# A one-token attention and FFN kernel: query weights at the front in long rows, another order for the K and V loads, and most of the output projection ahead of the last V blocks

## The chip, the cores and the metric

The kernel runs on one core of a Trainium2 chip. The metric is the device time of one execution in microseconds (us). Executions of a kernel agree here within some tenths of a per cent, so times are medians of several runs. A profile is one execution, and its span is some 2 us shorter than the time that is measured around it.

A 128 x 128 block product on PE (TensorE) is a pair of instructions: a weight load (PEld in the profile) and a matmul. DVE is VectorE, ACT is ScalarE, POOL is GpSimd, and SP is the sequencer that issues the loads.

## The reference

One token goes through grouped-query attention over a cache of 32768 positions and through a gated FFN, and a gate mixes the two.

```python
# x: 1 x 512; K and V caches: 8 groups x 32768 positions x 128 (64 MB each in bf16)
g = sigmoid((x * gate_w).sum(-1))
q = (x @ wq).reshape(32, 128)                 # 32 heads, 4 for each of 8 K/V groups
p = softmax(q @ k.T * 128 ** -0.5)            # for each head, k of its group
a = (p @ v).reshape(4096) @ wo                # wo: 4096 x 512
b = (silu(x @ w_gate) * (x @ w_up)) @ w_down  # 512 -> 1792 -> 512
out = g * a + (1 - g) * b
```

There is little arithmetic for each byte: 148 MB are read once, 134 MB of them K and V.

## The kernel before

K and V come in 128 blocks of 1 MB (4096 positions; each partition gets 32 positions, one row of 8 KB). PE transposes each K block, DVE and ACT copy the transposes to SBUF, and PE multiplies them with the four queries of the group. When a group's scores are complete, the maximum is taken (DVE, then an all-partition reduction on POOL), ACT exponentiates, and V blocks of that group are multiplied while the next group's K runs.

One list of jobs gives both the order of the loads and the order of the work on PE. In a group, four K blocks (six in the last) come before V starts:

```python
NKB = 5        # K buffers
NVB = 6        # V buffers
def vlag(g):
    return 6 if g == G - 1 else 4
# ... jobs: K(g,0..VL-1), then V(g-1,b) and K(g,b) in turn, then what is left of V(g-1)
jobs += [("V", G - 1, b) for b in range(NB)]
# on SP, for each job in turn:
if kind == "K":
    if b == 0:
        issue_wq(g)                            # 0.5 MB: this group's 512 columns, rows of 1 KB
    if ki >= NKB:
        sp.wait_ge(sem_fill, FPB * (ki - NKB + 1))
    sp.dma_start(kbuf[:, slot, :, :], ...)     # 1 MB
    if g == 0 and b == 3:
        issue_wf()                             # w_gate, w_up, w_down
else:
    if not wo_issued and g == G - 1:
        sp.wait_ge(sem_pe_b, 1)                # w_o overwrites the FFN weights
        sp.dma_start(wo_v, A_wo.rearrange("(h p) n -> p h n", p=128))
    ...
```

At the end, everything after the last V block is serial:

```python
pe.matmul(ps_e[:, 0:H], ones_f, esum2)         # sums of the exponentials over the partitions
# DVE: rS = 1 / ps_e;  oTs = ps_o * rS
for oc in range(OC):                           # 4 x 32 matmuls with w_o
    for h in range(H):
        pe.matmul(ps_m[:, M_A0 + oc : ...], wo_v[:, h, oc * 128 : (oc + 1) * 128], oTs[:, h : h + 1])
# DVE: diff = a - b; res = g * diff + b;  PE: 4 transposes to a row;  DVE: copy;  SP: store
```

## Time and profile before

| | before |
|---|---|
| time, median | 381.31 us |
| span of the profile | 379.5 us |
| PE busy, mean granted clock | 73%, 0.752 |
| read from HBM | 148.11 MB, 390 GB/s over the span |
| packets under 2 KB | 12230 of 29696 |
| last V block landed | 370.3 us |
| from there to the end | 9.1 us |

The page of the kernel before, in part: its first line, the row of PE's share, two rows of forty slices of the span (DMA busy in tenths, and GB/s), the packets, the queues, and the chain of waits that ended last.

```profile
span 379.5 us, 14143 instructions
...
PE 278.0 (73%) x6582; PEld 271.5 (72%) x6582; DVE 139.0 (37%) x233; ACT 99.9 (26%) x210; POOL 4.3 (1%) x17
...
DMA  7999999999999999999999999999999899999960
GB/s 283 401 381 417 407 420 415 419 405 417 419 420 412 414 415 421 413 408 421 415 421 406 418 419 418 414 408 420 419 416 410 359 376 421 415 366 383 420 273 4
DMA packets 29696, 149.02 MB, mean 393 GB/s; under 512 B 2243, under 2 KB 12230, under 8 KB 13254
...
q1 hardware_dynamic: 29638, 148.12, 96.3%
q8 instruction: 52, 0.85, 0.9%
...
DMA 44%; PE 40%; issue 11%; DVE 2%; SPq 1%; ACT 0%; POOL 0%; POOLq 0%
```

DMA is full from the second slice nearly to the end, so this is a kernel of loads. The tempting lines are the low slices (359 and 376 near 300 us). The windows by stage of the kernel before look at them closer; the columns are the stretch, the busy time of each engine with its instructions, the clock of PE, the DMA share of sixteen engines, and GB/s.

```profile
295.00:300.00 5.00, 1.88 (x51) 1.71 (x52) 0.00 (x0) 0.00 (x0) 0.00 (x0) 0.50 1.01 413
300.00:305.00 5.00, 5.00 (x87) 5.00 (x85) 2.47 (x5) 1.02 (x1) 0.00 (x0) 0.62 0.65 259
305.00:310.00 5.00, 4.93 (x123) 4.84 (x121) 4.96 (x10) 3.11 (x17) 0.37 (x1) 1.00 0.98 393
```

On average a third of the DMA engines stand idle from 300 to 305 us. In the last group six K loads are issued in a row into five buffers, and the sixth waits until PE has emptied the first. Whether that costs time is decided by another record of the trace: each large load's 16 landings, read here as one for each DMA engine. The table is made from those records (us from the span's start; "step" is the time since the last landing of the load before).

```
load    first   8th     13th    last    step of the last
K(0,0)    7.03    7.35    7.54    7.76
K(3,0)  125.20  128.14  128.57  130.07  3.81
K(3,1)  127.69  130.60  131.06  132.58  2.50
K(7,3)  297.67  302.42  305.85  307.19  2.55
K(7,4)  300.15  304.90  308.33  309.68  2.49
K(7,5)  308.40  308.94  310.82  312.18  2.49     <- 8.25 us after K(7,4), not 2.49
V(6,0)  310.89  311.42  314.57  314.85  2.68
w_o     345.22  345.74  348.90  349.17 11.90     4 MB
V(7,6)  362.71  363.15  366.39  367.84  2.48
V(7,7)  365.18  365.61  368.87  370.31  2.47
```

The landings of one load drift apart, from 0.7 us to 9.5 us. A load counts only when the last one is in. The last engine takes 2.49 us for each 1 MB load, with some longer steps like the 3.81, but it never stops: while the early engines stand idle for some 5.8 us (their landings of K(7,4) and K(7,5) are 8.25 us apart in place of 2.49), its step stays at 2.49 us.

The tail in the timeline of the kernel before (start, duration, engine, line, operation, tiles; in brackets the idle time before it):

```profile
370.36 1.02 PE L468 MATMUL ps_o<-ET,vbuf 128*128 128x4 bf16 x32 [1.45 <-DMA vbuf<-in_A_v_cache_dram]
...
371.24 0.61 PE L484 MATMUL pst<-esum,ones_f 128*128 128x32 f32 x2
371.89 0.36 DVE L658 RECIPROCAL rS<-pst 128x32 f32<-128x32 f32 x1 [37.88 <-PE pst L484]
372.28 0.19 DVE L661 TENSOR_TENSOR oTs<-ps_o,rS 128x32 bf16<-128x32 f32 x1
...
372.52 3.57 PE L495 MATMUL ps_m<-oTs,wfo 128*128 128x1 bf16 x128 [0.68 <-DVE oTs L661]
...
377.24 0.68 DVE L679 CAST res_row<-pst 1x512 bf16<-1x512 f32 x1 [0.68 <-PE pst L505]
377.94 0.27 SPq L323 DMA_DIRECT2D out_dram<-res_row  x1
```

PE is ready and waits 1.45 us for the last V block. Then 9.1 us of small steps follow, of which the 128 matmuls with w_o are the largest.

### The profile page before, as it was taken

To read this page: it belongs to the slowest core of one execution; us is meant where nothing else is said; L and a number is where in the kernel's file an instruction comes from. 1 tells how busy PE (TensorE), PEld (TensorE's weight loads), DVE (VectorE), ACT (ScalarE), POOL (GpSimd) and SP (SyncE) were. 2 spreads that over 40 slices of the span, in tenths; PEclk is the share of its full clock that TensorE was granted. 3 is DMA by queue.
4 is the path that set the end of the run, shared out by engine and by line. 5 is a ranking of instruction groups with operands and counts; after the bars stand their busy time and mean duration, and the time that the engine had idled before them with its cause. 6 is when DMAs were issued, how large, how long until landed. Compare 5 with 4: busy or idle time off the path is not lost.

```text
span 379.5 us, 14143 instructions
## 1 busy us (share of the span) xinstructions
PE 278.0 (73%) x6582; PEld 271.5 (72%) x6582; DVE 139.0 (37%) x233; ACT 99.9 (26%) x210; POOL 4.3 (1%) x17
## 2 busy tenths in 40 slices
PE   0469969886988698859898598958985697840345
PEld 0468969786988698859898598858985597830235
DVE  0226536330933184306722184205731194300001
ACT  1035561331533043403232143203332143410000
POOL 0000000000000000000000000000000000000000
PEclk9959967985988689966956598556987599855555
DMA  7999999999999999999999999999999899999960
GB/s 283 401 381 417 407 420 415 419 405 417 419 420 412 414 415 421 413 408 421 415 421 406 418 419 418 414 408 420 419 416 410 359 376 421 415 366 383 420 273 4
DMA packets 29696, 149.02 MB, mean 393 GB/s; under 512 B 2243, under 2 KB 12230, under 8 KB 13254
## 3 DMA queue, kind: packets, MB, share of 16 engines
q1 hardware_dynamic: 29638, 148.12, 96.3%
q8 instruction: 52, 0.85, 0.9%
q14 instruction: 6, 0.05, 0.0%
HBM read 148.11 MB, written 0.00 MB: 390 GB/s over the span
## 4 chain that ended last, share of the span: by engine, by line
DMA 44%; PE 40%; issue 11%; DVE 2%; SPq 1%; ACT 0%; POOL 0%; POOLq 0%
DMA kbuf<-in_A_k_cache_dram 35%; PE pst L449 24%; DMA vbuf<-in_A_v_cache_dram 10%; PE ps_sc L416 7%; PE ps_o L468 6%; SPq L314 1%; DVE ktT L627 1%; PE ps_m L495 1%; PE ps_m L368 1%; DVE pmaxf L609 0%; PE ps_m L381 0%; PE ps_m L354 0%; ACT ktT L552 0%; DVE res_row L679 0%; PE pst L505 0%
## 5 line engine op out<-in xcount | busy, mean ns | idle before, releaser
L449 PE MATMUL pst<-ident,kbuf 128*128 128x128 bf16 x2048 | 189.6, 247 | 24.0 <-ACT ktT L552 10.1
L627 DVE COPY ktT<-pst 128x1024 bf16<-128x1024 bf16 x188 | 125.3, 690 | 179.8 <-PE pst L449 179.6
L449 PEld LDWEIGHTS pst<-ident,kbuf 128*128 128x128 bf16 x2048 | 143.1, 111 | 27.1 <-issue 14.3
L552 ACT ACTIVATE ktT<-pst 128x1024 bf16<-128x1024 bf16 x68 | 69.6, 1024 | 190.1 <-PE pst L449 190.1
L468 PE MATMUL ps_o<-ET,vbuf 128*128 128x4 bf16 x2048 | 63.6, 168 | 49.7 <-DMA vbuf<-in_A_v_cache_dram 40.4
L416 PE MATMUL ps_sc<-qT,ktT 128*128 128x4 bf16 x2048 | 92.6, 167 | 6.2 <-issue 6.1
L468 PEld LDWEIGHTS ps_o<-ET,vbuf 128*128 128x128 bf16 x2048 | 58.9, 99 | 52.0 <-DMA vbuf<-in_A_v_cache_dram 28.3
L416 PEld LDWEIGHTS ps_sc<-qT,ktT 128*128 128x128 bf16 x2048 | 86.9, 102 | 6.2 <-issue 5.9
L536 ACT ACTIVATE ET<-ps_sc,nbias 128x128 bf16<-128x128 f32 x64 | 22.5, 377 | 0.2
L658 DVE RECIPROCAL rS<-pst 128x32 f32<-128x32 f32 x1 | 0.4, 357 | 37.9 <-PE pst L484 37.9
L536 ACT ACTIVATION_READ_ACCUMULATOR ET<-ps_sc,nbias 128x1 f32 x64 | 13.8, 216 | 0.0
L354 PE MATMUL ps_m<-xT,wqb 128*128 128x1 bf16 x128 | 4.8, 166 | 11.6 <-POOL ident L239 7.0
L354 PEld LDWEIGHTS ps_m<-xT,wqb 128*128 128x128 bf16 x128 | 4.1, 103 | 12.2 <-POOL ident L239 7.1
L609 DVE TENSOR_REDUCE pmaxf<-ps_sc 128x4 f32<-128x512 f32 x16 | 10.9, 681 | 0.4 <-PE ps_sc L416 0.4
L528 ACT ACTIVATE nbias<-gmax 128x4 f32<-128x4 f32 x8 | 1.6, 205 | 22.9 <-POOL gmax L254 22.9
L254 POOL PARTITION_ALL_REDUCE gmax<-pmax x8 | 3.0, 374 | 306.2 <-DVE pmax L613 306.2
L517 ACT ACTIVATE g_col<-gtot 128x1 f32<-128x1 f32 x1 | 0.2, 202 | 19.4 <-POOL gtot L249 19.4
L368 PE MATMUL ps_m<-xT,wfo 128*128 128x1 bf16 x112 | 3.2, 164 | 2.5 <-issue 2.5
L368 PEld LDWEIGHTS ps_m<-xT,wfo 128*128 128x128 bf16 x112 | 3.0, 99 | 2.6 <-issue 2.6
L495 PEld LDWEIGHTS ps_m<-oTs,wfo 128*128 128x128 bf16 x128 | 3.5, 104 | 0.8 <-DVE oTs L661 0.8
L495 PE MATMUL ps_m<-oTs,wfo 128*128 128x1 bf16 x128 | 3.6, 165 | 0.7 <-DVE oTs L661 0.7
L585 DVE CAST qT<-ps_m 128x4 bf16<-128x4 f32 x8 | 1.2, 153 | 7.0 <-PE ps_m L354 7.0
(36 smaller groups left out, 16.9 us busy)
## 6 DMA issues: line engine op xcount, KB each, us to landing
kbuf<-in_A_k_cache_dram SPq DMA_DIRECT2D x64, 1024.0 KB, 17.1
vbuf<-in_A_v_cache_dram SPq DMA_DIRECT2D x64, 1024.0 KB, 17.9
wqb<-in_A_wq_dram SPq DMA_DIRECT2D x8, 512.0 KB, 17.2
wfo<-in_A_wo_dram SPq DMA_DIRECT2D x1, 4096.0 KB, 23.3
wfo<-in_B_w_gate_dram SPq DMA_DIRECT2D x1, 1792.0 KB, 17.1
wfo<-in_B_w_up_dram SPq DMA_DIRECT2D x1, 1792.0 KB, 21.1
wfo<-in_B_w_down_dram SPq DMA_DIRECT2D x1, 1792.0 KB, 25.6
x_row<-in_A_x_dram SPq DMA_DIRECT2D x1, 1.0 KB
```

The costliest lines, as they stand in the source:

```text
L254: pool.partition_all_reduce(gmax[:, g, :], pmax[:, g, :], 128, ReduceOp.max).then_inc(sem_gmax, 1)
L314: sp.dma_start(vbuf[:, slot, :, :], A_v_cache[0, g, b * B : (b + 1) * B, :].rearrange("(p r) d -> p r d", r=R),).then_inc(sem_v_load[slot] ...
L354: ins = pe.matmul(ps_m[:, M_Q0 + h : M_Q0 + h + 1], wqb[:, slot, c, hl * DH : (hl + 1) * DH], xT[:, c : c + 1], start=(c == 0), stop=(c == ...
L368: ins = pe.matmul(ps_m[:, base + fc : base + fc + 1], wt[:, c, fc * 128 : (fc + 1) * 128], xT[:, c : c + 1], start=(c == 0), stop=(c == KC ...
L416: ins = pe.matmul(bank[:, col : col + HPG], ktT[:, slot, t * 128 : (t + 1) * 128], qT[:, g * HPG : (g + 1) * HPG], start=True, stop=True,)
L449: ins = pe.transpose(stb[:, t * 128 : (t + 1) * 128], kbuf[:, slot, r, :], ident[:, :],)
L468: ins = pe.matmul(ps_o[:, g * HPG : (g + 1) * HPG], vbuf[:, slot, r, :], ET[:, g, :, n], start=(n == 0), stop=(n == NT - 1),)
L495: ins = pe.matmul(ps_m[:, M_A0 + oc : M_A0 + oc + 1], wo_v[:, h, oc * 128 : (oc + 1) * 128], oTs[:, h : h + 1], start=(h == 0), stop=(h == ...
L536: act.activation(ET[:, g, h, bk * TPSB : (bk + 1) * TPSB], sc[:, h, :], ACT.Exp, bias=nbias[:, g, h : h + 1], scale=SCALE, accum_out=esum[ ...
L552: act.activation(ktT[:, j % NKT, :], pst[j % NST][:, :], ACT.Copy).then_inc(sem_cp_a, 1)
L609: dve.tensor_reduce(pmaxf[:, f, :], sc, AX.X, ALU.max).then_inc(sem_pmax, 1)
L627: dve.tensor_copy(ktT[:, j % NKT, :], pst[j % NST][:, :]).then_inc(sem_cp_d, 1)
```

## The change

Its intent: larger pieces for the weights that come in 1 KB rows, an order of loads that keeps more of them outstanding, and a shorter tail. Its core, with cuts:

```diff
-    NVB = 6
+    NVB = 8
     def vlag(g):
-        return 6 if g == G - 1 else 4
+        return 2
+    dma_jobs = []                      # an order of its own for the loads
+    for g in range(G):
+        for b in range(NB):
+            if g >= 1:
+                dma_jobs.append(("V", g - 1, b))
+            dma_jobs.append(("K", g, b))
+    dma_jobs += [("V", G - 1, b) for b in range(NB)]
 ...  # SP: all of wq at the front, rows of 8 KB; PE: q of all heads at once
+                for c in range(KC):
+                    sp.dma_start(wq_v[:, c, :], A_wq[c * 128 : (c + 1) * 128, :])
 ...  # w_down in rows of 14 KB; the FFN's columns are dealt to match
-                        wd, B_w_down.rearrange("(c p) n -> p c n", p=128)
+                        wd, B_w_down.rearrange("(p c) n -> p c n", p=128)
-                                    wt[:, c, fc * 128 : (fc + 1) * 128],
+                                    wt[:, c, :].rearrange("p (q f) -> p q f", f=FC)[:, :, fc],
 ...  # w_o right after, into the place of wq
+                    sp.wait_ge(sem_pe_q, 1)
+                    sp.dma_start(wo_v, A_wo.rearrange("(h p) n -> p h n", p=128))
 ...  # PE, ahead of the V blocks of the last group
+                        if g == G - 1 and b == 0:
+                            emit_S(0, G - 1)              # sums of groups 0 to 6
+                            emit_wo(M_A0, 0, HE)          # 28 of 32 heads: 112 matmuls
+                        if g == G - 1 and b == 5:
+                            emit_S(G - 1, G)              # sums of group 7
                         if b == 0:
+                            pe.wait_ge(sem_exp, 2 * HPG * g + HPG)   # half of the group
+                        if b * R == TPSB:
                             pe.wait_ge(sem_exp, 2 * HPG * (g + 1))
 ...  # after the last V block only the last group's 16 matmuls are left
+                emit_wo(M_A1, HE, H)
```

To make room, the exponentials of three groups are kept (they were kept for all eight), and VectorE's part of the tail is split in the same way.

More of the change, by code (lines that the diff above doesn't have):

```diff
@@ L60, in bass_gated_mix__gqa_block_cached__swiglu_ffn__decode_kernel @@
     LAG = 3
-    NWQ = 2
+    NEG = 3
     SCALE = float(DH) ** -0.5
@@ L123, in bass_gated_mix__gqa_block_cached__swiglu_ffn__decode_kernel, with _check_orders @@
     assert len(jobs) == 2 * G * NB
+    dma_jobs = []
[5 more added lines that the diff above has]
+    dma_jobs += [("V", G - 1, b) for b in range(NB)]
+    assert sorted(dma_jobs) == sorted(jobs)
+    def _check_orders():
+        issued_k = issued_v = 0
+        cons_k = cons_v = 0
+        di = 0
+        pi = 0
+        nK = sum(1 for j in dma_jobs if j[0] == "K")
+        progress = True
+        while pi < len(jobs) and progress:
+            progress = False
+            while di < len(dma_jobs):
+                kind = dma_jobs[di][0]
+                if kind == "K" and issued_k - cons_k < NKB:
+                    issued_k += 1
+                elif kind == "V" and issued_v - cons_v < NVB:
+                    issued_v += 1
+                else:
+                    break
+                di += 1
+                progress = True
+            kind = jobs[pi][0]
+            if kind == "K" and cons_k < issued_k:
+                cons_k += 1
+                pi += 1
+                progress = True
+            elif kind == "V" and cons_v < issued_v:
+                cons_v += 1
+                pi += 1
+                progress = True
+        assert pi == len(jobs), f"static schedule deadlocks at pe job {pi} / dma job {di}"
+    _check_orders()
     with ExitStack() as es:
@@ L130, in bass_gated_mix__gqa_block_cached__swiglu_ffn__decode_kernel @@
         sem_v_load = [S_(f"s_v_load{i}") for i in range(NVB)]
-        sem_wq_load = [S_(f"s_wq_load{i}") for i in range(NWQ)]
+        sem_ld_wq = S_("s_ld_wq")
         sem_fill = S_("s_fill")
@@ L190, in bass_gated_mix__gqa_block_cached__swiglu_ffn__decode_kernel @@
         WF = 2 * KC * F + FC * NOUT
-        assert H * NOUT <= WF
         wfo = T("wfo", [128, WF], BF16)
@@ L195, in bass_gated_mix__gqa_block_cached__swiglu_ffn__decode_kernel @@
         wd = wfo[:, 2 * KC * F : WF].rearrange("p (c n) -> p c n", c=FC)
-        wo_v = wfo[:, 0 : H * NOUT].rearrange("p (h n) -> p h n", h=H)
-        wqb = T("wqb", [128, NWQ, KC, HPG * DH], BF16)
+        WQO = max(KC * H * DH, H * NOUT)
+        wqo = T("wqo", [128, WQO], BF16)
+        wq_v = wqo[:, 0 : KC * H * DH].rearrange("p (c n) -> p c n", c=KC)
+        wo_v = wqo[:, 0 : H * NOUT].rearrange("p (h n) -> p h n", h=H)
         kbuf = T("kbuf", [128, NKB, R, DH], BF16)
@@ L200, in bass_gated_mix__gqa_block_cached__swiglu_ffn__decode_kernel @@
         ktT = T("ktT", [128, NKT, TPF * 128], BF16)
-        ET = T("ET", [128, G, HPG, NT], BF16)
+        ET = T("ET", [128, NEG, HPG, NT], BF16)
         pmaxf = T("pmaxf", [128, NSB, HPG], FP32)
@@ L210, in bass_gated_mix__gqa_block_cached__swiglu_ffn__decode_kernel @@
         b_col = T("b_col", [128, OC], FP32)
+        pre_col = T("pre_col", [128, OC], FP32)
         diff_col = T("diff_col", [128, OC], FP32)
@@ L227, in bass_gated_mix__gqa_block_cached__swiglu_ffn__decode_kernel @@
         M_A0 = M_B0 + OC
-        assert M_A0 + OC <= 512
+        M_A1 = M_A0 + OC
+        M_E0 = M_A1 + OC
+        assert M_E0 + H <= 512
+        HE = H - HPG
         ps_e = pst[0][:, :].bitcast(FP32)
@@ L261, in _, with issue_weights @@
                 sp.dma_start(gw_row[0:1, :], gate_w.unsqueeze(0)).then_inc(sem_ld_x, 16)
-                def issue_wq(g):
-                    slot = g % NWQ
-                    if g >= NWQ:
-                        sp.wait_ge(sem_pe_q, g - NWQ + 1)
+                for c in range(KC):
                     sp.dma_start(
-                        wqb[:, slot, :, :],
-                        A_wq[:, g * HPG * DH : (g + 1) * HPG * DH].rearrange(
-                            "(c p) n -> p c n", p=128
-                        ),
-                    ).then_inc(sem_wq_load[slot], 16)
-                def issue_wf():
+                        wq_v[:, c, :], A_wq[c * 128 : (c + 1) * 128, :]
+                    ).then_inc(sem_ld_wq, 16)
+                def issue_weights():
                     sp.dma_start(
@@ L281, in issue_wf @@
                     sp.dma_start(
-                        wd, B_w_down.rearrange("(c p) n -> p c n", p=128)
+                        wd, B_w_down.rearrange("(p c) n -> p c n", p=128)
                     ).then_inc(sem_ld_wf, 16)
+                    sp.wait_ge(sem_pe_q, 1)
+                    sp.dma_start(
+                        wo_v, A_wo.rearrange("(h p) n -> p h n", p=128)
+                    ).then_inc(sem_ld_wo, 16)
                 ki = 0
                 vi = 0
-                wo_issued = False
-                for kind, g, b in jobs:
+                for kind, g, b in dma_jobs:
                     if kind == "K":
-                        if b == 0:
-                            issue_wq(g)
                         slot = ki % NKB
@@ L301, in _ @@
                         ki += 1
-                        if g == 0 and b == min(3, NB - 1):
-                            issue_wf()
-                    else:
-                        if not wo_issued and g == G - 1:
-                            sp.wait_ge(sem_pe_b, 1)
-                            sp.dma_start(
-                                wo_v, A_wo.rearrange("(h p) n -> p h n", p=128)
-                            ).then_inc(sem_ld_wo, 16)
-                            wo_issued = True
+                        if g == 0 and b == 3:
+                            issue_weights()
+                    else:
                         slot = vi % NVB
@@ L320, in _ @@
                         vi += 1
-                assert wo_issued and ki == G * NB and vi == G * NB
+                assert ki == G * NB and vi == G * NB
                 sp.wait_ge(sem_dve_row, 1)
@@ L340, in _ @@
                 pe.wait_ge(sem_ident, 1)
-                def emit_q(g):
-                    slot = g % NWQ
-                    pe.wait_ge(sem_wq_load[slot], 16 * (g // NWQ + 1))
-                    if g == 0:
-                        pe.wait_ge(sem_dve_x, 2)
-                    else:
-                        pe.wait_ge(sem_dve_qT, g)
-                    if g == 2:
-                        pe.wait_ge(sem_dve_bcol, 1)
-                    for hl in range(HPG):
-                        h = g * HPG + hl
-                        for c in range(KC):
-                            ins = pe.matmul(
-                                ps_m[:, M_Q0 + h : M_Q0 + h + 1],
-                                wqb[:, slot, c, hl * DH : (hl + 1) * DH],
-                                xT[:, c : c + 1],
-                                start=(c == 0),
-                                stop=(c == KC - 1),
-                            )
-                    ins.then_inc(sem_pe_q, 1)
+                pe.wait_ge(sem_dve_x, 2)
+                pe.wait_ge(sem_ld_wq, 16 * KC)
+                for h in range(H):
+                    for c in range(KC):
+                        ins = pe.matmul(
+                            ps_m[:, M_Q0 + h : M_Q0 + h + 1],
+                            wq_v[:, c, h * DH : (h + 1) * DH],
+                            xT[:, c : c + 1],
+                            start=(c == 0),
+                            stop=(c == KC - 1),
+                        )
+                ins.then_inc(sem_pe_q, 1)
                 def emit_ffn():
@@ L403, in emit_scores @@
                         sc_group_started.add(g)
-                        pe.wait_ge(sem_dve_qT, g + 1)
+                        if g == 0:
+                            pe.wait_ge(sem_dve_qT, 1)
                     wait_copy(j)
@@ L427, in emit_scores, with emit_S, emit_wo @@
                         emit_outb()
+                def emit_S(g0, g1):
+                    pe.wait_ge(sem_dve_esum2, 1 if g0 == 0 else 2)
+                    pe.matmul(
+                        ps_m[:, M_E0 + g0 * HPG : M_E0 + g1 * HPG],
+                        ones_f[:, :],
+                        esum2[:, g0:g1, :].rearrange("p g h -> p (g h)"),
+                        start=True,
+                        stop=True,
+                    ).then_inc(sem_pe_S, 1)
+                def emit_wo(base, h0, h1):
+                    pe.wait_ge(sem_dve_oTs, 1 if h0 == 0 else 2)
+                    pe.wait_ge(sem_ld_wo, 16)
+                    for oc in range(OC):
+                        for h in range(h0, h1):
+                            ins = pe.matmul(
+                                ps_m[:, base + oc : base + oc + 1],
+                                wo_v[:, h, oc * 128 : (oc + 1) * 128],
+                                oTs[:, h : h + 1],
+                                start=(h == h0),
+                                stop=(h == h1 - 1),
+                            )
+                    ins.then_inc(sem_pe_a, 1)
                 kuse = [0] * NKB
@@ L436, in _ @@
                     if kind == "K":
-                        if b == 0:
-                            emit_q(g)
                         slot = ki % NKB
@@ L470, in _ @@
                                 vbuf[:, slot, r, :],
-                                ET[:, g, :, n],
+                                ET[:, g % NEG, :, n],
                                 start=(n == 0),
@@ L481, in _ @@
                 assert next_scores == NF and vi == G * NB
-                pe.wait_ge(sem_dve_esum2, 1)
-                pe.matmul(
-                    ps_e[:, 0:H],
-                    ones_f[:, :],
-                    esum2[:, :, :].rearrange("p g h -> p (g h)"),
-                    start=True,
-                    stop=True,
-                ).then_inc(sem_pe_S, 1)
-                pe.wait_ge(sem_dve_oTs, 1)
-                pe.wait_ge(sem_ld_wo, 16)
-                for oc in range(OC):
-                    for h in range(H):
-                        ins = pe.matmul(
-                            ps_m[:, M_A0 + oc : M_A0 + oc + 1],
-                            wo_v[:, h, oc * 128 : (oc + 1) * 128],
-                            oTs[:, h : h + 1],
-                            start=(h == 0),
-                            stop=(h == H - 1),
-                        )
-                ins.then_inc(sem_pe_a, 1)
+                emit_wo(M_A1, HE, H)
                 pe.wait_ge(sem_dve_res, 1)
@@ L520, in emit_sg @@
                     act.wait_ge(sem_pe_h, 1)
-                    act.wait_ge(sem_dve_qT, 2)
+                    act.wait_ge(sem_dve_qT, 1)
                     act.activation(
@@ L531, in emit_exps @@
                     act.wait_ge(sem_nbias, g + 1)
+                    if g >= NEG:
+                        act.wait_ge(sem_v_free, NB * (g - NEG + 1))
                     for bk in range(2):
@@ L536, in emit_exps @@
                             act.activation(
-                                ET[:, g, h, bk * TPSB : (bk + 1) * TPSB],
+                                ET[:, g % NEG, h, bk * TPSB : (bk + 1) * TPSB],
                                 sc[:, h, :],
@@ L581, in _ @@
                 )
-                def emit_qcopy(g):
-                    dve.wait_ge(sem_pe_q, g + 1)
-                    dve.tensor_copy(
-                        qT[:, g * HPG : (g + 1) * HPG],
-                        ps_m[:, M_Q0 + g * HPG : M_Q0 + (g + 1) * HPG],
-                    ).then_inc(sem_dve_qT, 1)
+                dve.wait_ge(sem_pe_q, 1)
+                dve.tensor_copy(qT[:, :], ps_m[:, M_Q0 : M_Q0 + H]).then_inc(sem_dve_qT, 1)
                 def emit_t():
@@ L615, in emit_pmax @@
                         ).then_inc(sem_pmax, 1)
-                emit_qcopy(0)
                 next_f = 0
-                next_qg = 1
                 t_done = False
@@ L629, in _ @@
                         )
-                    if next_qg < G and j >= next_qg * FPG:
-                        emit_qcopy(next_qg)
-                        next_qg += 1
                     if not t_done and j >= J_DVE_T:
@@ L641, in _ @@
                         next_f += 1
-                while next_qg < G:
-                    emit_qcopy(next_qg)
-                    next_qg += 1
                 if not t_done:
@@ L651, in _, with emit_rS @@
                     next_f += 1
-                dve.wait_ge(sem_exp, 2 * HPG * G)
-                dve.tensor_tensor(
-                    esum2[:, :, :], esum[:, :, 0, :], esum[:, :, 1, :], ALU.add
-                ).then_inc(sem_dve_esum2, 1)
-                dve.wait_ge(sem_pe_S, 1)
-                dve.reciprocal(rS[:, :], ps_e[:, 0:H]).then_inc(sem_dve_rS, 1)
-                dve.wait_ge(sem_dve_rS, 1)
-                dve.wait_ge(sem_v_free, G * NB)
-                dve.tensor_tensor(oTs[:, :], ps_o[:, 0:H], rS[:, :], ALU.mult).then_inc(
+                def emit_rS(g0, g1):
+                    k = 1 if g0 == 0 else 2
+                    dve.wait_ge(sem_exp, 2 * HPG * g1)
+                    dve.tensor_tensor(
+                        esum2[:, g0:g1, :], esum[:, g0:g1, 0, :], esum[:, g0:g1, 1, :], ALU.add
+                    ).then_inc(sem_dve_esum2, 1)
+                    dve.wait_ge(sem_pe_S, k)
+                    dve.reciprocal(
+                        rS[:, g0 * HPG : g1 * HPG],
+                        ps_m[:, M_E0 + g0 * HPG : M_E0 + g1 * HPG],
+                    ).then_inc(sem_dve_rS, 1)
+                    dve.wait_ge(sem_dve_rS, k)
+                emit_rS(0, G - 1)
+                dve.wait_ge(sem_v_free, (G - 1) * NB)
+                dve.tensor_tensor(oTs[:, 0:HE], ps_o[:, 0:HE], rS[:, 0:HE], ALU.mult).then_inc(
                     sem_dve_oTs, 1
@@ L665, in _ @@
                 dve.tensor_tensor(
-                    diff_col[:, :], ps_m[:, M_A0 : M_A0 + OC], b_col[:, :], ALU.subtract
+                    pre_col[:, :], ps_m[:, M_A0 : M_A0 + OC], b_col[:, :], ALU.subtract
                 ).then_inc(sem_dve_diff, 1)
+                emit_rS(G - 1, G)
+                dve.wait_ge(sem_v_free, G * NB)
+                dve.tensor_tensor(oTs[:, HE:H], ps_o[:, HE:H], rS[:, HE:H], ALU.mult).then_inc(
+                    sem_dve_oTs, 1
+                )
+                dve.wait_ge(sem_pe_a, 2)
                 dve.wait_ge(sem_dve_diff, 1)
+                dve.tensor_tensor(
+                    diff_col[:, :], ps_m[:, M_A1 : M_A1 + OC], pre_col[:, :], ALU.add
+                ).then_inc(sem_dve_diff, 1)
+                dve.wait_ge(sem_dve_diff, 2)
                 dve.wait_ge(sem_act_g, 1)
```

## The prediction

> **What bounds the kernel now.** The DMA stream: on the page its row stands at 9 from the second slice to the 37th, queue 1 uses 96.3% of sixteen engines' span, and the chain of waits is mostly K and V loads (35% and 10%). PE is 73% busy at a mean clock of 0.752: slack. The trace's landing records say more. A load is done only when its 16 landings are in (the Trainium skill, "DMA: Bandwidth & Descriptors", section on why a DMA increments its semaphore by 16; every load here shows 16). First and last landing are 0.7 us apart at the start and drift to 9.5 us at 300 us; I put that to the 52 instruction fetches of 16 KB (1.07 us each) falling on some engines only. So the last engine sets the time. Its landings step by 2.49 us per 1 MB, without a hole, from 5 to 370.3 us. The dip in the windows by stage (300 to 305 us: 259 GB/s, DMA share 0.65) is the early engines running dry; the last one keeps its step. Removing that dip should gain nearly nothing.
>
> **What the change does.**
> 1. wq in four 1 MB loads with 8 KB rows, not eight 0.5 MB loads with 1 KB rows. An old load takes 1.45 us of the stream, as many K bytes 1.24 us: 8 x 0.2 = 1.6 us gained.
> 2. w_down with 14 KB rows: 5.2 us now, 4.4 us at K's rate: 0.8 us gained.
> 3. w_o moves to the front, still in 1 KB rows, 12 us before and after: 0.
> 4. K and V interleaved from a group's start, 8 V buffers, V two blocks behind, half-group waits for the exponentials: more room ahead, but there was no hole to fill: 0. Exponentials end about 4.5 us after the row maximum; PE has the next K block meanwhile.
> 5. q for all heads at once: PE waits for 4 MB (to 14 us), then 128 small matmuls (5 us). Loads are queued behind: 0.
> 6. Strided FFN weight loads: off the critical path.
> 7. The tail. From the last V block (370.4) to the end (379.5): V 1.0, sum over partitions 0.6, reciprocal 0.4, oTs 0.2, 128 output matmuls 3.6, then 3.3 of small steps and the store. Sum, reciprocal and 112 output matmuls move under DMA time; the remaining 16 take about 0.6: 3.8 us gained, all critical.
>
> **Sum.** 1.6 + 0.8 + 3.8 = 6.2 of 381.3: 375.1 us, range 372.5 to 378.5. Faster by over 2% (below 373.7): 0.17; within 2%: 0.81; slower: 0.02.
>
> **What would show each step right or wrong.** Last V landing at 367.9, not 370.3 (1, 2); last V block to end 5.3 us, not 9.1 (7); no dip at 300 us, with the last engine's step still 2.5 us (4); packets under 2 KB falling from 12,230 to about 6,340; PE's waits naming mostly K and V loads.
>
> **What would make it wrong.** The last engine not being the bound: then the dip's 2 us come back too and the time is near 373. Another number of fetches on the worst engine: 1.3 us each way. PE reaching the last V blocks late, with 112 output matmuls and half clock before them: 1 to 2 us lost. PE falling behind in the steady part (a K and V pair takes it 3.5 us at full and 5.3 us at half clock, against 5.0 us of DMA), which 13 buffers should absorb.

## The result, and the profile after

The changed kernel takes 375.37 us (median of 8 runs) against 381.38 us (13 runs of the kernel before): a ratio of 0.9844, interval 0.9834 to 0.9854. The prediction was 375.1 us.

The page of the changed kernel, the same parts:

```profile
span 373.4 us, 14148 instructions
...
PE 296.5 (79%) x6584; PEld 291.7 (78%) x6584; DVE 142.3 (38%) x230; ACT 99.9 (27%) x210; POOL 4.3 (1%) x17
...
DMA  7999999999999999999999999999999999999971
GB/s 282 418 411 410 347 409 419 420 418 418 420 417 416 418 419 417 416 421 416 419 414 420 419 417 419 420 417 419 420 418 417 416 419 420 417 420 418 377 310 41
DMA packets 24383, 149.01 MB, mean 399 GB/s; under 512 B 2179, under 2 KB 6278, under 8 KB 7302
...
q1 hardware_dynamic: 24326, 148.12, 96.8%
q8 instruction: 51, 0.84, 0.9%
...
DMA 53%; PE 36%; SPq 6%; issue 3%; DVE 1%; ACT 1%; POOL 0%; DVEq 0%
```

The order of loads did what it was meant to do: the slices are level, and the one low slice left before the last blocks (347) is w_o with its 1 KB rows, now at 38 to 50 us. Packets under 2 KB fell by half. The windows by stage of the changed kernel, where the dip was:

```profile
295.00:300.00 5.00, 4.15 (x123) 4.05 (x120) 2.38 (x4) 2.05 (x2) 0.00 (x0) 1.00 1.01 416
300.00:305.00 5.00, 4.38 (x96) 4.29 (x96) 2.08 (x3) 1.02 (x1) 0.00 (x0) 0.66 1.01 418
305.00:310.00 5.00, 3.46 (x51) 3.46 (x52) 0.69 (x1) 1.28 (x2) 0.00 (x0) 0.50 1.01 421
```

The landing records of the changed kernel, however, show that the last engine's step is what it was:

```
load    first   8th     13th    last    step of the last
wq 0      5.80    5.92    6.15    6.50
wq 3     13.26   13.40   13.76   14.37  2.48
w_down   36.54   36.69   38.03   38.52  4.42     before: 5.16
w_o      48.50   48.64   50.00   50.44 11.92     before: 11.90
V(6,0)  299.47  303.66  307.35  308.98  2.48
K(7,0)  301.96  306.15  309.84  311.47  2.48
V(7,6)  357.25  358.32  363.56  365.36  2.67
V(7,7)  359.72  360.79  366.04  367.84  2.48
```

The spread now grows to 11.0 us, since the early engines are free to run further ahead; nothing is gained by that. The last V block lands at 367.84 us, 2.47 us earlier than before. The tail in the timeline of the changed kernel:

```profile
365.48 0.65 PE L524 MATMUL ps_o<-ET,vbuf 128*128 128x4 bf16 x19 [2.62 <-issue]
...
366.41 2.70 PE L524 MATMUL ps_o<-ET,vbuf 128*128 128x4 bf16 x96
...
369.22 0.16 DVE L704 TENSOR_TENSOR oTs<-ps_o,rS 128x4 bf16<-128x4 f32 x1 [2.45 <-PE ps_o L524]
...
369.44 0.59 PE L471 MATMUL ps_m<-oTs,wqo 128*128 128x1 bf16 x16 [0.33 <-DVE oTs L704]
...
371.16 0.68 DVE L723 CAST res_row<-pst 1x512 bf16<-1x512 f32 x1 [0.68 <-PE pst L542]
371.87 0.26 SPq L357 DMA_DIRECT2D out_dram<-res_row  x1
```

The 3.57 us of output matmuls became 0.59 us, and the sum and the reciprocal are gone from here. From the last landing to the end it is 373.38 - 367.84 = 5.54 us, against 379.46 - 370.31 = 9.15 us before: 3.61 us less. The two gains add up to 2.47 + 3.61 = 6.08 us; the spans differ by 6.1. PE comes to the last block late: shortly before, from 362.85 us, it stood still for 2.62 us, for nothing that the profile names ("issue"), and three V blocks are then worked off in one run (96 matmuls), so the last is done 1.27 us after it landed.

What that stop was comes out when PE's instructions are counted in the trace. After 25 us PE's weight loads stop six times for over 0.4 us with the mark "issue", each time a multiple of 256 instructions apart (before the records no. 2498, 2754, 4290, 4802, 12737 and 12994 of PE's two rows, give or take one). Each time they go on 1.2 to 1.5 us after an instruction fetch of 16 KB (queue q8) has ended; the one for this stop ran from 363.1 to 364.2 us. So PE waited for its own instructions. Without this stop it would have been in time: it was in the fifth of the last group's eight V blocks, a block takes it 1.0 us, and the seventh landed at 365.36 us (an estimate from these numbers).

### The profile page after: what moved, and what is told of

It is laid out like the page before. It is cut to its first block, busy times and chain, and to the rows that moved or that the text cites. A ratio compares the mean times of both kernels' runs of the same rounds, so it can differ in the third digit from the quotient of the medians.

```text
span 373.4 us, 14148 instructions
## 1 busy us (share of the span) xinstructions
PE 296.5 (79%) x6584; PEld 291.7 (78%) x6584; DVE 142.3 (38%) x230; ACT 99.9 (27%) x210; POOL 4.3 (1%) x17
## 4 chain that ended last, share of the span: by engine, by line
DMA 53%; PE 36%; SPq 6%; issue 3%; DVE 1%; ACT 1%; POOL 0%; DVEq 0%
DMA kbuf<-in_A_k_cache_dram 53%; PE pst L498 21%; PE ps_o L524 7%; PE ps_sc L443 5%; SPq L320 3%; PE ps_m L394 2%; SPq L317 2%; PE ps_m L471 1%; SPq L335 1%; SPq L310 1%; ACT ET L575 0%; PE ps_m L407 0%; DVE ktT L660 0%; ACT L575 0%; SPq L324 0%
## 5 line engine op out<-in xcount | busy, mean ns | idle before, releaser
L498 PE MATMUL pst<-ident,kbuf 128*128 128x128 bf16 x2048 | 206.4, 262 | 49.7 <-DMA kbuf<-in_A_k_cache_dram 43.6
L660 DVE COPY ktT<-pst 128x1024 bf16<-128x1024 bf16 x188 | 128.3, 691 | 193.6 <-PE pst L498 193.1
L498 PEld LDWEIGHTS pst<-ident,kbuf 128*128 128x128 bf16 x2048 | 155.8, 117 | 51.6 <-DMA kbuf<-in_A_k_cache_dram 46.3
L443 PEld LDWEIGHTS ps_sc<-qT,ktT 128*128 128x128 bf16 x2048 | 91.5, 106 | 3.1 <-issue 2.9
L380 PE MATMUL ps_m<-xT,wqo 128*128 128x1 bf16 x128 | 3.5, 165 | 11.8 <-DMA wqo<-in_A_wq_dram 11.8
L380 PEld LDWEIGHTS ps_m<-xT,wqo 128*128 128x128 bf16 x128 | 3.5, 104 | 11.8 <-issue 11.8
L565 ACT ACTIVATE nbias<-gmax 128x4 f32<-128x4 f32 x8 | 1.6, 205 | 23.2 <-POOL gmax L300 23.2
L394 PE MATMUL ps_m<-xT,wfo 128*128 128x1 bf16 x112 | 6.9, 198 | 0.0
L394 PEld LDWEIGHTS ps_m<-xT,wfo 128*128 128x128 bf16 x112 | 6.8, 158 | 0.0
L471 PE MATMUL ps_m<-oTs,wqo 128*128 128x1 bf16 x128 | 3.7, 165 | 1.0 <-DVE oTs L695 0.6
L471 PEld LDWEIGHTS ps_m<-oTs,wqo 128*128 128x128 bf16 x128 | 3.6, 104 | 1.2 <-DVE oTs L695 0.8
```

The lines of the kernel that those rows point to most:

```text
L380: ins = pe.matmul(ps_m[:, M_Q0 + h : M_Q0 + h + 1], wq_v[:, c, h * DH : (h + 1) * DH], xT[:, c : c + 1], start=(c == 0), stop=(c == KC - 1),)
L394: ins = pe.matmul(ps_m[:, base + fc : base + fc + 1], wt[:, c, :].rearrange("p (q f) -> p q f", f=FC)[:, :, fc], xT[:, c : c + 1], start=( ...
L443: ins = pe.matmul(bank[:, col : col + HPG], ktT[:, slot, t * 128 : (t + 1) * 128], qT[:, g * HPG : (g + 1) * HPG], start=True, stop=True,)
L471: ins = pe.matmul(ps_m[:, base + oc : base + oc + 1], wo_v[:, h, oc * 128 : (oc + 1) * 128], oTs[:, h : h + 1], start=(h == h0), stop=(h = ...
L498: ins = pe.transpose(stb[:, t * 128 : (t + 1) * 128], kbuf[:, slot, r, :], ident[:, :],)
L660: dve.tensor_copy(ktT[:, j % NKT, :], pst[j % NST][:, :]).then_inc(sem_cp_d, 1)
```

## The experiments

Theory A, that of the prediction: the last DMA engine and the serial tail after it set the time; the rows and the tail gave the gain, the new order and the eight buffers gave nothing. Rival B: the new order gave some 2 us by filling the dip at 300 us, and the rows or the tail gave less than was reckoned.

### One part at a time

Four runs take the change apart. **e1** puts the new tail alone into the kernel before (the two insertions of `emit_S` and `emit_wo`, the half-group waits, and VectorE's split).

> The kernel before with the new tail alone (sum over partitions, reciprocal and 112 of the 128 output matmuls ahead of the last V blocks; exponentials awaited by half groups). Theory A (the last DMA engine sets the time, and the tail after it is serial): the last V landing stays at 370.3 us, from there to the end about 5.5 us instead of 9.1: 377.7 us, 3.6 less than before. Rival B (part of the gain of the tail is given back, because the 112 matmuls delay the last V blocks, and the rest of the whole gain comes from the order of the loads): gain of 2.5 us or less. The dip at 300 us stays under both.

**e2** has the rows alone: the changed kernel with the old order, six V buffers and the old tail. (wq and w_o stay at the front, and q is still computed at once.)

```diff
-    NVB = 8
+    NVB = 6
-        return 2
+        return 6 if g == G - 1 else 4
+    dma_jobs = list(jobs)
-                            emit_S(0, G - 1)
-                            emit_wo(M_A0, 0, HE)
 ...
-                emit_wo(M_A1, HE, H)
+                emit_S(0, G)
+                emit_wo(M_A0, 0, H)
```

> The longer rows alone (wq in four loads of 8 KB rows at the front with all of q, w_down in 14 KB rows with the strided weight loads, w_o at the front), with the old tail, the old order of K and V, 6 V buffers. A: last V landing near 367.9 us, tail still 9.1: 378.9 us, 2.4 less than before. B: 1 us or less gained, since the rows were never the matter. The dip of the early engines may move or vanish as w_o and wq no longer stand in the middle; under A that changes nothing in the time.

**e3** has the order alone: the kernel before with `NVB = 8`, `vlag` 2 and the new `dma_jobs`.

> The kernel before with only the new order of loads (V and K alternating from the start of a group), V two blocks behind on PE and 8 V buffers. A: the dip near 300 us vanishes, the last engine's landings keep their 2.49 us step, and the time is that of before within 0.5 us (381.3). B: the dip was lost time, so 379.3 or less.

**e4** is the changed kernel with the old order and six V buffers (the first three edits of e2).

> The changed kernel with the old order of loads, V four and six blocks behind, 6 V buffers; rows and tail as changed. A: the time of the changed kernel within 0.5 us (375.4). B: slower than the changed kernel by 2 us or more (377.4). If it is slower and the tail after the last landing is longer, the order helps the tail and not the stream.

| kernel | time, median | ratio to before (interval) | last V landing | from there to the end |
|---|---|---|---|---|
| before | 381.54 us | | 370.31 | 9.15 |
| e1, tail alone | 377.78 | 0.9902 (0.9887 to 0.9917) | 370.87 | 5.3 |
| e2, rows alone | 379.09 | 0.9937 (0.9921 to 0.9954) | 367.65 | 9.1 |
| e3, order alone | 381.44 | 1.0004 (0.9988 to 1.0021) | 369.96 | 9.1 |
| e4, changed, old order | 375.34 | 0.9839 (0.9825 to 0.9854) | 368.02 | 5.3 |

(Times from the rounds, landings from the profiles; the row "before" has its profile from the first section.) By the medians the tail gives 3.8 us and the rows 2.5 us; the order's 0.1 us is within the noise. Together that is 6.3 us, and the changed kernel gained 6.0. No run has the longer rows without the new places of wq and w_o. That the place is not what counts is read from w_o, which moved to the front with its rows unchanged and takes 11.92 us there against 11.90. The windows by stage of e3 show the dip filled, with no gain:

```profile
300.00:305.00 5.00, 4.49 (x100) 4.41 (x98) 0.76 (x2) 0.77 (x1) 0.00 (x0) 0.50 1.01 418
305.00:310.00 5.00, 4.43 (x67) 4.35 (x65) 3.52 (x6) 1.88 (x11) 0.37 (x1) 0.50 1.02 418
```

In e4 the early engines' landings are 7.9 us apart at 310 us, so they stand idle there as in the kernel before, and the time is that of the changed kernel. Rival B falls in both directions.

### Why one engine is last

The prediction put the drift of the landings to instruction fetches (queue q8: 52 of 16 KB). **e5** adds instructions and nothing else: memsets of one byte on GpSimd, which is idle.

```diff
+        scratch = T("scratch", [1, 2320], mybir.dt.uint8)
                 for g in range(G):
+                    for i in range(290 * g, 290 * (g + 1)):
+                        pool.memset(scratch[:, i : i + 1], 0)
                     pool.wait_ge(sem_pmax, 3 * (g + 1))
```

> The changed kernel with 2320 one-byte memsets more on the idle GpSimd (290 ahead of each group's row maximum, about 29 us of each 42 us), which compute nothing. At the 51 fetches of 16 KB that 14148 instructions brought, they should bring some 8 or 9 more. If fetches make the late engines late (about 1.3 us each on the engine they fall on, eight engines), the last V landing moves by 1.3 to 2.6 us, to 369 or 370.5, and the time to about 377. If the lateness has another cause, the time stays at 375.4. A longer wait for the row maximum, seen in the waits for POOL, would spoil the test.

It took 378.07 us (ratio 0.9907, 0.9892 to 0.9921), 2.7 us more than the changed kernel (2.4 by the ratios, since the two ran in different rounds), and its last V block landed at 370.32 us, 2.48 later. The wait for the row maximum hardly moved (ACT waits 24.5 us for it in all, 23.2 in the changed kernel). The queues of the changed kernel and of e5, one fence for each:

```profile
q8 instruction: 51, 0.84, 0.9%
q14 instruction: 6, 0.05, 0.0%
```

```profile
q8 instruction: 51, 0.84, 0.9%
q14 instruction: 24, 0.20, 0.1%
```

The expectation was right in sign and size but wrong in the path. The number of 16 KB fetches stayed. They go with PE's instructions: there is one for each 256 of PE's 13,269 records. GpSimd's instructions came by another queue in pieces of 8 KB (18 more within the span, 0.15 MB, which is 64 bytes for each memset).

The last engine's landings show the fetches one by one. The changed kernel has six steps of 3.5 to 3.85 us in place of 2.49, some 50 us apart. A 16 KB fetch starts every six to seven us, so that one stands near each step proves little. But the six steps fall exactly at every eighth fetch (the 9th, 17th, 25th, 33rd, 41st and 49th of 51), and so do five of the kernel before (from the 17th to the 49th of 52).

In e5 the last engine's record has none of these six. After 50 us it has fifteen other long K and V steps, thirteen of 3.12 to 3.18 us and two of 3.4 to 3.5, and no run without the memsets shows such a row. There is one such step for each of the fifteen 8 KB fetches that were added in that stretch, within 1 to 3 us of its start. So another engine comes last in e5, one that seems to carry all the added fetches: 18 x 0.65 us are some 12 us (an estimate), against 10.0 us by which the K and V steps over 2.6 us exceed the usual one in the changed kernel. The end moved by 2.48.

So a fetch delays the engine that carries it by about 0.65 us (8 KB) or 1.35 us (16 KB). In the kernel before, the last engine's nine K and V steps of over 2.7 us lie 8.6 us above the usual step in all; not each of them has such a fetch beside it. The trace doesn't number the engines, so that the fetches fall on some engines only, and that the 16 KB ones take turns over eight, is inferred from the landings.

### Trying to move work from the late engines to the early ones

If half of the engines are early (8 landings of the last V block are in by 360.8 us, 7 us before the last), they could carry more. **e6** loads half of w_o by eight loads of 8 partitions.

```diff
-                    sp.dma_start(wo_v, A_wo.rearrange("(h p) n -> p h n", p=128))
+                    wo_src = A_wo.rearrange("(h p) n -> p h n", p=128)
+                    sp.dma_start(wo_v[0:64], wo_src[0:64])
+                    for p0 in range(64, 128, 8):
+                        sp.dma_start(wo_v[p0 : p0 + 8], wo_src[p0 : p0 + 8])
```

> The changed kernel with half of w_o (64 partitions, 2 MB) loaded by eight loads of 8 partitions. The Trainium skill (DMA: Bandwidth & Descriptors, on how many engines a load gets) says that such a load runs on the lowest-numbered eight of the sixteen. That takes 3 us of w_o's 12 from one half of the engines and gives it to the other. If the half that is late (by 8 to 11 us at the end) is the upper one, the last V landing comes about 3 us earlier: 372.4. If it is the lower one, about 3 us later: 378.4. If all engines share one limit and the last engine is not special, the time stays at 375.4.

414.32 us, ratio 1.0853: none of the three answers expected. The small loads were slow in themselves. The row of GB/s of e6 shows it between the fourth slice and the ninth:

```profile
GB/s 293 420 408 310 148 61 78 99 195 419 420 419 416 416 420 416 418 419 416 419 418 415 418 419 420 418 417 420 416 420 416 418 419 419 416 419 418 397 318 23
```

Their landings stretch from about 50 to 91 us, some 5 us for each 256 KB, SP stands 41.7 us in issuing the eight, and the K loads queue behind. Each small load adds 9 updates to its semaphore, where a large one adds 16. In e9 one of the nine comes right after the issue and eight come with the data, so these loads did run on eight engines; which eight, the trace doesn't show. **e9** avoids what seemed the reasons (1 KB rows, neighbouring partitions): one V block as sixteen loads of 8 partitions, 16 apart, in 8 KB rows.

```diff
+                        if (g, b) in V8:               # V8 = {(1, 3)}
+                            for p0 in range(16):
+                                sp.dma_start(vbuf[p0:128:16, slot, :, :], v_src[p0:128:16])
```

> The changed kernel with one V block (group 1, block 3) loaded by sixteen loads of 8 partitions each, 16 apart, with 8 KB rows. The eight-engine loads of w_o were slow in themselves (1 KB rows, 8 neighbouring partitions), so they told nothing of the balance. By the skill's rule these run on the lowest-numbered eight engines: 64 KB, or 2.5 us, less for one half and 2.5 us more for the other. If the late half is the upper one: last V landing 2.5 us earlier (365.3) and the time 372.9. If it is the lower one: 2.5 us later, 377.9. If these loads are slow in themselves again, the last engine's landings show a hole near that block.

384.17 us (its runs from 381.57 to 384.97), ratio 1.0047. The block that should have taken 5 us took about 15 us, and the windows by stage of e9 have a hole there:

```profile
115.00:120.00 5.00, 2.54 (x57) 2.45 (x52) 2.18 (x5) 2.68 (x4) 0.37 (x1) 0.89 1.03 231
120.00:125.00 5.00, 4.99 (x113) 4.93 (x110) 3.41 (x5) 2.73 (x16) 0.00 (x0) 0.77 1.03 228
```

The last V block landed at 377.43 us, 9.6 later than in the changed kernel, although its first landing was 9.7 us ahead of it. That agrees with theory A: the last landing of a K load is 9.6 us later than in the changed kernel from 131 us on, and still 9.6 at the end, while the first landing is at most 4.3 us later. But the question put, which half is late and whether it can be relieved, stays open. Why these loads are slow is open too: the loads of one MB run at 422 GB/s (1.05 MB in 2.485 us), these together at about 70.

### A shorter tail

**e7** tries two cuts in the tail: the last V block in two loads, so that fewer matmuls follow the last landing, and a result stored straight from its 128 x 4 tile without transposes.

```diff
+                        if vi == G * NB - 1:
+                            sp.dma_start(vbuf[:, slot, 0:24, :], v_src[:, 0:24, :])
+                            sp.dma_start(vbuf[:, slot, 24:R, :], v_src[:, 24:R, :])
-                                wo_v[:, h, oc * 128 : (oc + 1) * 128],
+                                wo_v[:, h, :].rearrange("p (q o) -> p q o", o=OC)[:, :, oc],
-                sp.dma_start(out[0, :, :], res_row[0:1, :])
+                sp.dma_start(out[0, 0, :].rearrange("(p o) -> p o", o=OC), res_col[:, :])
```

> The changed kernel with a shorter tail: the last V block in two loads (24 and 8 of its 32 rows of each partition), so that PE has 8 matmuls and not 32 after the last landing, and the output columns so dealt to the partitions that the result is stored straight from its 128 x 4 tile, without the 4 transposes and the row copy. After the last landing now 5.5 us: 1.3 of PE (0.25 of it waiting), 4 transposes 0.6, copy 0.7. Expected: 0.75 and 1.3 less, the strided output weights 0.2 to 0.5 more, the store of 128 pieces of 8 bytes perhaps 0.3 more: about 373.9, last landing unchanged at 367.8.

376.45 us, ratio 0.9867: 1.1 us slower than the changed kernel. The timeline of e7:

```profile
366.27 2.70 PE L537 MATMUL ps_o<-ET,vbuf 128*128 128x4 bf16 x96
...
370.48 0.35 SPq L366 DMA_DIRECT2D out_dram<-res_col  x1
```

The store is issued 1.4 us earlier than in the changed kernel, but its last landing is at 373.98 us: 3.5 us for 128 pieces of 8 bytes, against 1.1 us for one row of 1 KB (371.87 to 372.98). And the split gained nothing, because PE came late to the last block here as well, after the same stop of 2.62 us. **e8**, e6 and e7 together: ratio 1.0795, which says only what e6 says.

> Both edits of the two runs before this one together. If the late engines are the upper half, the gains add up, since one moves the last landing and the other what follows it: about 371. If they are the lower half, about 377.

Where does PE come in time? In e4, where the timeline shows it waiting for the last V block:

```profile
368.07 1.02 PE L517 MATMUL ps_o<-ET,vbuf 128*128 128x4 bf16 x32 [1.78 <-DMA vbuf<-in_A_v_cache_dram]
```

So **e10** takes the old order (which costs nothing, as e4 showed), keeps the store as a row, splits the last V block, folds g * (a of 28 heads - b) + b into one column beforehand, and copies the final row in halves on VectorE and ScalarE. **e11** is the changed kernel again, in the same rounds.

```diff
 # on e4
+                dve.scalar_tensor_tensor(diff_col, pre_col, g_col[:, 0:1], b_col, ALU.mult, ALU.add)
 ...
-                dve.tensor_tensor(diff_col, ps_m[:, M_A1 : M_A1 + OC], pre_col, ALU.add)
-                dve.scalar_tensor_tensor(res_col, diff_col, g_col[:, 0:1], b_col, ALU.mult, ALU.add)
+                dve.scalar_tensor_tensor(res_col, ps_m[:, M_A1 : M_A1 + OC], g_col[:, 0:1], diff_col, ALU.mult, ALU.add)
-                dve.tensor_copy(res_row[0:1, :], ps_r[0:1, 0:NOUT])
+                dve.tensor_copy(res_row[0:1, 0 : NOUT // 2], ps_r[0:1, 0 : NOUT // 2])
+                act.activation(res_row[0:1, NOUT // 2 : NOUT], ps_e[0:1, NOUT // 2 : NOUT], ACT.Copy)
```

> The changed kernel in the old order (the run before last of the first four, where PE stands idle 1.8 us ahead of the last V block, while in the changed kernel it comes to it late), with the last V block in two loads of 24 and 8 rows, the gate and the FFN's part folded beforehand into one column so that one VectorE step of 0.2 us goes, and the final row copied in halves by VectorE and ScalarE from two PSUM banks. Expected: 0.75 less PE after the last landing (8 matmuls for 32), 0.2 for the step, 0.3 for the copy: 1.2 us, to 374.1, with the last landing still near 368.0.

> The changed kernel as it is, on the same chip and in the same rounds as the trimmed one, to compare the two: 375.4 us, 1.2 more than the trimmed one.

e10 takes 374.21 us (ratio 0.9808, 0.9794 to 0.9821), e11 375.58 us (0.9843, 0.9829 to 0.9856): e10 is 1.4 us faster and the fastest kernel here, correct like all the others. The timeline of e10:

```profile
367.53 1.01 PE L530 MATMUL ps_o<-ET,vbuf 128*128 128x4 bf16 x32 [0.89 <-DMA vbuf<-in_A_v_cache_dram]
...
369.50 0.22 DVE L725 SCALAR_TENSOR_TENSOR res_col<-ps_m,g_col,diff_col 128x4 bf16<-128x4 f32 x1 [0.68 <-PE ps_m L475]
...
370.40 0.37 ACT L612 ACTIVATE res_row<-pst 1x256 bf16<-1x256 f32 x1 [24.76 <-PE pst L548]
370.40 0.41 DVE L730 CAST res_row<-pst 1x256 bf16<-1x256 f32 x1 [0.68 <-PE pst L548]
370.86 0.26 SPq L361 DMA_DIRECT2D out_dram<-res_row  x1
```

PE starts on the first 24 rows as they land and is done 0.4 us after the last landing (368.13 us); from that landing to the end it is 4.2 us, against 5.3 in e4.

## Why the prediction was right

- **The bound.** It was read from the landings of the last engine, not from the mean of sixteen. That decided the question of the dip: on the page it looks like 2 us of lost bandwidth, and e3 filled it for nothing (1.0004). The Trainium skill ("DMA: Bandwidth & Descriptors", on why a DMA increments its semaphore by 16) says that the engines of a load finish independently and that only the full count means the data is there. The traces agree: 16 landings for each large load, 0.7 to 11 us apart. (The prediction says this of every load; the two of 1 KB at the start have two landings each.)
- **Steps 1 and 2, the rows.** Predicted 2.4 us; the last landing moved by 2.47, e2 gained 2.45. wq's loads now step by 2.48 us for each MB, w_down's by 4.42 us where it was 5.16. The division is less exact than the sum. Between these two profiles w_down gave 0.74 us as predicted, but wq is in only 0.6 us earlier (14.37 against 14.96), not 1.6, since the start takes longer with loads of 1 MB. Another 1.2 us stands in w_gate's step (5.70 and 4.51), whose rows did not change; in e1 and e3, with the old rows, that step is 4.69 and 4.54. So single steps vary by about 1 us from profile to profile, and that the sum fits to 0.1 us is in part luck. The gain itself is not: the last V landing is at 369.96 to 370.87 us in three profiles with the old rows, and at 367.65 to 368.13 in six with the new (e5, e6, e8 and e9 left out, which disturb the loads).
- **Steps 3 and 4, w_o's place and the order.** Predicted 0. w_o steps by 11.92 us at the front and 11.90 before; the order alone gave 0.1 us, within its interval.
- **Step 5, q at once.** PE waits 11.8 us for wq, and no load waits for PE in that phase: the last engine's steps for K stay at 2.5 to 2.9 us.
- **Step 6, strided weight loads.** They cost PE more than thought of: 158 ns each at the median for 96. The granted clock is not the reason: they take 158 or 159 ns at 1.00 (at 71.6 us) and at 0.50 (74 to 78 us) alike. The FFN's 112 matmuls fall at 72 to 78 us, where the stream doesn't depend on them. The groups by source line, before and after:

```profile
L368 PEld LDWEIGHTS ps_m<-xT,wfo x112: 95/96/108, 49.6 to 55.1; 128*128 128x128 bf16 x112
```

```profile
L394 PEld LDWEIGHTS ps_m<-xT,wfo x112: 138/158/159, 71.6 to 78.3; 128*128 128x128 bf16 x112
```

- **Step 7, the tail.** Predicted 3.8 us, measured 3.61 in the profiles. The rest is what the prediction named as a danger: PE comes late to the last V block, after a stop of 2.62 us. It cost 0.2 us (V done 1.27 us after the landing, 1.07 before), not 1 to 2. The prediction put it to the 112 matmuls and the half clock; the trace puts it to the wait for instructions. In e1, where PE waits for the last block, the tail alone gave 3.8 us.
- **What was inferred and not shown** when the prediction was made: that instruction fetches cause the drift. e5 and the count of fetches support it, with the path corrected.

## What to carry to other kernels

In a kernel that is bound by loads, look for the engine that lands last and follow its steps: a dip in the mean bandwidth costs nothing while that engine goes on, and buffers or orders that only let the others run ahead gain nothing. What counts then is what every byte costs on that engine (here 1 KB rows against 8 KB rows) and what stands after its last landing. Take the tail apart step by step, put everything that doesn't need the last data ahead of it, and check that the engine that receives the last data is idle when it comes, or shortening its last piece of work gains nothing. An engine that stops under "issue" at equal counts of instructions may be waiting for them: look for an instruction fetch just before it goes on.

## What the Trainium skill lacked or had wrong

- "DMA: Bandwidth & Descriptors", Specifications: its smallest transfer for line rate is 512 B. Here rows of 1 KB were slower than rows of 8 KB: 0.52 MB in 1.45 us against 1.05 MB in 2.485 us (363 and 422 GB/s), and 4.19 MB of w_o in 11.9 us (352 GB/s).
- The same page gives about 358 GB/s as HBM's limit for a core, and says under Bandwidth that with the pair's other core idle one core gets more. Here one core held 415 to 421 GB/s over most of the span, so the figure of the table is too low for a core that runs alone.
- The same page, on how many engines a load gets, has no cost for few engines. Rates by number of partitions do stand elsewhere in the skill, and these runs were not made to test them. Loads of 8 partitions ran at about 70 GB/s together (e9: 1 MB in some 15 us).
- No page that I read says that instruction fetches slow the data loads: a fetch of 16 KB takes about 1.35 us from the engine that carries it (inferred from the landings), and 18 more fetches of 8 KB, for 2320 instructions of an idle engine, cost 2.7 us of the kernel's time (e5).
- No page that I read has a figure for a store in very small pieces: 3.5 us from issue to last landing for 128 pieces of 8 bytes (e7), 1.1 us for one of 1 KB (the changed kernel).
